# A fused attention and feed-forward kernel: a load, a set of copies and two value products change places

## The chip, the cores and the metric

The kernel runs on one core of a Trainium2 chip. The metric is device time in microseconds (us) of one execution; lower is better. Names of engines in the profile: PE is TensorE (matmuls; PEld its weight loads), DVE is VectorE, ACT is ScalarE, POOL is GpSimd, SP is SyncE. ACT, SP and Pool also issue transfers.

## The reference

Block-sorted attention over 4 batches, 8 heads, 768 positions and 64 features, and then a gated feed-forward layer on its output. Cut to what matters:

```python
P = sort_net                                   # (4, 8, 8, 8)
for _ in range(5):
    P = exp(P - max(P, -1)); P = P / (sum(P, -1) + 1e-9); P = P / (sum(P, -2) + 1e-9)
k_sorted = einsum('bhij,bhjcd->bhicd', P, k_blocks)      # 8 blocks of 96 positions
v_sorted = einsum('bhij,bhjcd->bhicd', P, v_blocks)
attn = softmax(q_blocks @ k_sorted.T / 8)                # inside each block
x = (attn @ v_sorted) as (3072, 512)
h = x @ w_in                                             # 512 -> 2048
out = (h * cos(h)) @ w_out                               # 2048 -> 512
```

## The kernel before

The work is cut into eight chunks of 384 tokens: chunk n is batch n // 2 and one half of its eight blocks. In a chunk the four blocks are `u` = 0 to 3. For each (n, u) the kernel calls `qk` (scores into PSUM; DVE takes the row maximum at L483 and subtracts it at L489), `expo` (ACT's exponential into one of three buffers `p_buf`, L507, then the transpose of the result: on PE for early chunks, otherwise by a transfer on SP's queue, L520), `av` (the value product on PE, L546; DVE divides by the sum, L553 and L555; the result is transposed by SP, L561, or on PE by `x_transpose`, L573). Then come `moe_up` (L597, with ACT's sine at L604 and DVE's product at L612) and `moe_down` (L629). The order of all instructions is written out by hand: each engine executes its own in that order, and the up and down products of one chunk carry, in slots between their matmuls, the attention calls of later chunks. `moe_down(n, slots, mid=...)` makes six halves of eight matmuls, e = 0 to 5; the calls in slot e follow half e, those in `mid[e]` stand behind its first four matmuls.

The head has an order of its own. Three loads bring the sort matrix into the tile `P_a` (L83 twice, L85 once); groups g = 0 and 1 are batches 0, 1 and 2, 3. DVE takes the maximum (L239), ACT the exponential (L240), and four rounds follow (`it` = 0 to 3): exponential on ACT (L330), a product with a mask on PE (`product`, L261), reciprocal and scaling on DVE (L350, L321, L324). Between the products of the rounds PE also transposes q of chunk 0 (`q_products`, `q_turn`, L299; 32 transposes, 16 in each of two PSUM tiles), which ACT copies out. At the end of the rounds `spread(0)` writes the sorting matrix `bds[0]` (L280). From it `k_sort_0` makes the sorted keys of chunk 0: per call some products on PE (L361) and four copies into `kT[0]`, of 8 or 16 columns per head, on DVE (V, L288) or ACT (A, L286). `v_turn` turns the matrix for the values (tile `bdv`), and `v_sort_b` sorts the values (L451).

Pool issues the loads of q, k, v and the weights (`load_q`, `load`, `load_w_in`, `load_w_out`), clears buffers and makes the identity (`make_identity`); it also permutes v (L176). PSUM tiles come from two pools: `big` with three buffers (B in the calls) and `acc` with two (C).

Of the kernel before, what the change touches and what calls it, by code (L numbers as in the profile page):

```python
# [18 lines left out]
def kernel(  # L19
# [15 lines left out]
    nc = tc.nc  # L35
    B, H, S, D = q.shape
# [26 lines left out]
    big = ctx.enter_context(tc.tile_pool(name="big", bufs=3, space=bass.MemoryType.PSUM))  # L63
# [7 lines left out]
    vbuf, kbuf = kv[:, :CD], kv[:, CD:]  # L71
# [10 lines left out]
    for r, b in ((64, 0), (0, 1)):  # L82
        (nc.scalar, nc.sync)[b].dma_start(  # L83
            out=P_a[r:r + 64, 0], in_=sort_net[b].rearrange("h i j -> (h i) j"))
    nc.scalar.dma_start(  # L85
        out=P_a[:, 1], in_=sort_net[2:].rearrange("b h i j -> (b h i) j"))

    kin_d = k.rearrange("b h (j c) d -> b (h j) (c d)", j=nb)
    vin_d = v.rearrange("b h (j c) d -> b (h j) (c d)", j=nb)

    def load(buf, r, src):
        nc.gpsimd.dma_start(out=buf[r:r + 64], in_=src)
# [16 lines left out]
    def q_zeroed(n):  # L109

        return kbuf[:blk, :2 * (QZ + D)] if n % 2 else q_mem[:]
# [7 lines left out]
    def load_q(n):  # L119
        b, ih = n // 2, n % 2  # L120
        if n < NQ:

            nc.gpsimd.dma_start(
                out=q_rows, in_=q[b][:, ih * IC * blk:(ih + 1) * IC * blk].rearrange(
                    "h (p r) d -> p h (r d)", r=QR))
        else:
            src = q[b].rearrange("h (i c) d -> c i h d", c=blk).rearrange(
                "c i (h e) d -> c i h e d", e=2)
            q_heads = q_zeroed(n).rearrange("p (e x) -> p e x", e=2)[:, :, :QZ].rearrange(
                "p e (i h w) -> p i h e w", i=IC, h=H2)[:, :, :, :, :D]  # L130
            for i in range(IC):
                for e in range(2):
                    nc.gpsimd.dma_start(  # L133
                        out=q_heads[:, i, :, e], in_=src[:, ih * IC + i, :, e])

    def q_of(n, e):
        return q_turned[n % 2][:, e]
# [17 lines left out]
    def load_w_in(z):  # L155
        c = slice(z * Dff // 4, (z + 1) * Dff // 4)
        nc.gpsimd.dma_start(out=w_in_t[:, :, c], in_=w_in_d[:, :, c])

    def load_w_out(z):
        c = slice(z * FC // 4, (z + 1) * FC // 4)  # L160
        nc.gpsimd.dma_start(out=w_out_t[:, c], in_=w_out_d[:, c])
# [22 lines left out]
    kTs = const.tile([128, 3, 3, NB, HT], BF16, name="kTs")  # L184
    kT, kT2 = [kTs[:, :, 0], kTs[:, :, 2]], kTs[:, :, :2]

    load_q(0)
    make_identity(nc, ident[:])
    load(kbuf, 64, kin_d[0])
    load(vbuf, 0, vin_d[0])  # L190
    NP = 3
    p_bufs = []
    for i in range(NP):
        t = const.tile([blk, 2 * H2, 128], BF16, name=f"p_buf{i}")
        nc.gpsimd.memset(t[:, :, blk:], 0.0)
        p_bufs.append(t)
    vS[0] = const.tile([blk, 4 * NB, VW], BF16, name="vS")
    vS[1] = pair[:blk].rearrange("p (x w) -> p x w", w=VW)

# [59 lines left out]
    def product(lhs, rhs):  # L259
        ps = acc.tile([128, nb], FP32, name="sk", tag="acc")  # L260
        nc.tensor.matmul(  # L261
            ps[:], lhs.rearrange("p x j -> p (x j)"), rhs, start=True, stop=True)
        return ps
# [15 lines left out]
    def spread(g):  # L279
        nc.vector.scalar_tensor_tensor(  # L280
            bds[g][:], maskp.to_broadcast([128, 2 * H, nb]), ci[g][:], along(T[g]),
            op0=ALU.mult, op1=ALU.mult)

    def copy_on(eng, dst, src):
        if eng is nc.scalar:
            eng.copy(dst, src)  # L286
        else:
            eng.tensor_copy(dst, src)  # L288

    V, A = nc.vector, nc.scalar  # L290
# [3 lines left out]
    def q_products(n, z, lo, hi, pool, tag):  # L294
        if lo == 0:
            q_ps[n, z] = pool.tile([128, 2, IC, QR, blk // QR], BF16, name="qps", tag=tag)
        for i in range(lo, hi):
            e, hp, r = i // (2 * QR), i // QR % 2, i % QR
            nc.tensor.transpose(  # L299
                q_ps[n, z][hp * D:(hp + 1) * D, e, :, r],  # L300
                q_rows[:, (z * 2 + e) * 2 + hp, r * D:(r + 1) * D], ident[:blk, :blk])

    def q_turn(n, z, pool, tag, lo=0):
        q_products(n, z, lo, 4 * QR, pool, tag)
        ps = q_ps.pop((n, z))

        def place(hp, rows):
            dst = q_of(n, hp)[rows, :QW].rearrange("d (i h c) -> d h i c", h=H2, c=blk)
            return dst[:, z * 2:z * 2 + 2], ps[rows].rearrange("d e i r p -> d e i (r p)")

        if n == 0:
            return [place(0, slice(0, 128))]
        return [place(hp, slice(hp * D, (hp + 1) * D)) for hp in range(2)]
# [5 lines left out]
    def balance(g):  # L319

        nc.vector.scalar_tensor_tensor(  # L321
            T_eps[g][:], E_eps[g][:], 1.0, rr_one[g][:], op0=ALU.mult, op1=ALU.mult,
            accum_out=cs[g][:])
        nc.vector.reciprocal(ci[g][:], cs[g][:])  # L324
# [3 lines left out]
    for it in range(4):  # L328
        for g in range(NG):
            nc.scalar.activation(E[g], T[g], AF.Exp, scale=ci[g][:])  # L330
        nc.vector.tensor_copy(seen[:], E[0][:, :1])
        if it == 3:
            copy_on(A, *turned[0])
        sk = [product(same, E[g]) for g in range(NG)]
        if it == 1:
            q_products(0, 0, 0, 10, big, "big")
        elif it == 2:
            turned = q_turn(0, 0, big, "big", 10)
            q_products(0, 1, 0, 4, big, "big")
        elif it == 3:  # L340
            turned = q_turn(0, 1, big, "big", 4)
            copy_on(A, *turned[0])
        if it == 1:

            nc.gpsimd.tensor_copy(held[:], cs[1][:])
            for z in range(3):
                load_w_in(z)
            load_w_out(0)
        for g in range(NG):
            nc.vector.reciprocal(rr[g], sk[g][:])  # L350
            if it < 3 or g == 0:
                balance(g)
                if it == 3:
                    spread(0)
# [5 lines left out]
    def k_products(ps, t, c, rows, rhs, keys=kbuf):  # L360
        nc.tensor.matmul(  # L361
            ps[:, t], keys[rows, c * 2 * D:(c + 1) * 2 * D], rhs, start=True, stop=True)

    def k_sort_0(t0, nt, eng, pool, tag):

        ps = pool.tile([128, nt, 2 * MH], FP32, name="ks", tag=tag)
        for t in range(nt):
            k_products(ps, t, t0 + t, slice(64, 128),
                       bds[0][64:, H:, :IC])
        ms, ts = slice(0, MH), slice(t0, t0 + nt)  # L370
        psv = ps.rearrange("p t (e m) -> p e m t", e=2)
        for hp in range(2):
            for x in range(2):
                copy_on(eng, kT[0][hp * D:(hp + 1) * D, hp + x, ms, ts],
                        psv[x * D:(x + 1) * D, hp])
# [58 lines left out]
    def v_turn(eng=A):  # L434
        ps = big.tile([128, 128], FP32, name="bdp", tag="big")
        for r in (0, 64):
            nc.tensor.matmul(
                ps[r:r + 64], ident[:, 64 - r:128 - r], bds[0].rearrange("p x i -> p (x i)"),
                start=True, stop=True)
        copy_on(eng, bdv.rearrange("p x i -> p (x i)"), ps[:])  # L440
# [217 lines left out]
    def moe_down(n, slots=(), stores=nc.sync, mid={}):  # L658

        for e in range(2 * TC // 128):  # L660
            down(n, e // 2, e % 2, stores, mid.get(e, ()))
            step(slots[e] if e < len(slots) else ())

    B, C = (big, "big"), (acc, "acc")
# [27 lines left out]
        next(wz)  # L692

    k_sort_0(40, 8, V, *B)
    k_sort_0(0, 16, V, *C)
    v_turn()
    load_q(1)
    k_sort_0(32, 8, V, *B)
    load_w_in(3)
    k_sort_0(16, 16, A, *B)  # L700
    v_sort_b(0, 0, 8, A, *B)
    load_w_out(1)
    qk(0, 0)
# [140 lines left out]
    def ahead(n, *more):  # L844
# [5 lines left out]
        for e, calls in more:  # L850
# [8 lines left out]
             mid={5: [(x_transpose, 3, 1, V, *B), (x_transpose, 3, 2, V, *B),  # L859
                  (x_transpose, 3, 3, V, *B)]})  # L860
# [13 lines left out]
             None, mid={5: [(x_transpose, 4, 3, A, *B)]})  # L874
# [5 lines left out]
               [(qk_half, 5, 2, 1)], [], [(qk, 5, 3)]])  # L880
    expo(5, 1)
    expo(5, 2)
    moe_down(4, [[(qk, 6, 0)], [(av, 5, 0), (expo, 5, 3)], [(qk, 6, 1)],
                 [(av, 5, 2), (expo, 6, 0)], [(av, 5, 3, True), (expo, 6, 1), (qk, 6, 2)]],
             None, mid={3: [(av, 5, 1)], 5: [(x_transpose, 5, 3, A, *B)]})
    q_transpose_dma(7)
# [6 lines left out]
             mid={5: [(x_transpose, 6, 3, A, *B)]})  # L893
# [1 line left out]
               [(qk_half, 7, 3, 1)]])  # L895
    expo(7, 2)
    expo(7, 3)
    moe_down(6, [[(av, 7, 0)], [(av, 7, 1)], [(av, 7, 2, True)], [(av, 7, 3, True)],
                 [(x_transpose, 7, 2, A, *B)]], None,
             mid={5: [(x_transpose, 7, 3, A, *B)]})  # L900
    moe_up(7, [[(let_go, 6, 0)], [(let_go, 6, 1)], [(let_go, 6, 2)]])
    for e in range(2 * TC // 128 - 2):
        down(7, e // 2, e % 2, nc.sync)
# [41 lines left out]
```

## Time and profile before

| | |
|---|---|
| median of 3 runs | 239.96 us (239.51 to 241.65) |
| profiled execution | 241.18 us, of which the span of the profile is 239.4 us |
| busy, share of the span | PE 226.0 us (94%), DVE 175.8 (73%), ACT 155.3 (65%), POOL 87.7 (37%) |
| transfers | 30.90 MB, mean 129 GB/s |
| granted clock of TensorE | 0.998 of full speed |

The profile is that of one execution. Times in its rows count from the start of the span. A row of the order in time gives start, length, engine, line, operation, tiles and count; in brackets stands the idle time of the engine before it, and what ended that. The chain of waits is followed back from the last instruction: at each step to what released it.

### The profile page before, as it was taken

Reading aid. Unit: us, or ns where it says so; the run is one execution under the profiler, and the core shown is the slowest. Engines: PE = TensorE matmul, PEld = TensorE weight load, DVE = VectorE, ACT = ScalarE, POOL = GpSimd, SP = SyncE. Lnnn points to the kernel's source line nnn. Section 1 sums busy time; section 2 is a strip of 40 time slices with the busy share of each in tenths; the row PEclk is TensorE's granted clock in tenths of the full one; section 3 lists DMA queues with packets and bytes.
Section 4 is the critical chain, followed back from the end, with each engine's and each line's share of the span. In section 5 each row is a group of like instructions: output and inputs, shape, how many; then the busy total and the mean of one; then the engine's idle time right before and its main releaser. Section 6 shows DMA issues by size and latency. Waiting matters only on the chain.

```text
span 239.4 us, 5344 instructions
## 1 busy us (share of the span) xinstructions
PE 226.0 (94%) x2148; PEld 148.1 (62%) x2169; DVE 175.8 (73%) x325; ACT 155.3 (65%) x217; POOL 87.7 (37%) x110
## 2 busy tenths in 40 slices
PE   2797999999999999999999999999999999999994
PEld 0777788956766566656566565655565566456554
DVE  3678977698879976895768986897789769635700
ACT  4355967785688946888578947683667376737611
POOL 6469953896960056990726200800000000000000
PEclk9999999999999999999999999999999999999999
DMA  6999999992999259786889769926671450251012
GB/s 82 213 198 205 207 210 219 212 158 89 132 152 162 66 138 191 122 179 154 117 115 126 79 136 140 189 43 99 136 212 33 102 181 0 49 140 44 0 47 89
DMA packets 66681, 30.90 MB, mean 129 GB/s; under 512 B 55392, under 2 KB 62176, under 8 KB 66400
## 3 DMA queue, kind: packets, MB, share of 16 engines
q0 software_dynamic: 24048, 13.64, 41.1%
q1 hardware_dynamic: 42096, 16.72, 29.8%
q8 instruction: 17, 0.28, 0.5%
q10 hardware_dynamic: 512, 0.20, 0.3%
q14 instruction: 8, 0.07, 0.1%
HBM read 27.27 MB, written 6.29 MB: 140 GB/s over the span
## 4 chain that ended last, share of the span: by engine, by line
PE 85%; DVE 7%; DMA 3%; ACT 2%; issue 1%; ACTq 0%; DVEq 0%
PE h L597 34%; PE o L629 31%; PE sc L428 4%; PE av L546 4%; PE ks L361 2%; DVE kTs L288 2%; PE xps L573 2%; PE pps L533 2%; PE vs L461 2%; DMA P_a<-in_sort_net_dram 2%; PE o L909 1%; PE sk L261 1%; PE qps L299 1%; DMA vperm<-p_buf 1%; PE vs L451 1%
## 5 line engine op out<-in xcount | busy, mean ns | idle before, releaser
L597 PE MATMUL h<-xT,w_in_t 128*128 128x384 bf16 (+1 forms) x576 | 91.2, 310 | 0.4 <-DVE xn L555 0.3
L629 PE MATMUL o<-w_out_t,gg 128*128 128x512 bf16 x347 | 85.1, 379 | 1.1
L604 ACT ACTIVATE c<-h,half_pi 128x768 f32<-128x768 f32 (+1 forms) x68 | 58.6, 864 | 26.8 <-PE h L597 25.6
L612 DVE TENSOR_TENSOR gg<-c,h 128x768 bf16<-128x768 f32 (+1 forms) x64 | 57.1, 899 | 22.2 <-ACT c L604 22.2
L597 PEld LDWEIGHTS <-w_in_t 128*128 128x128 bf16 x576 | 53.1, 98 | 27.1 <-issue 1.0
L629 PEld LDWEIGHTS <-gg 128*128 128x128 bf16 x368 | 33.1, 98 | 30.9
L489 DVE TENSOR_TENSOR s<-sc,mx 96x384 f32<-96x384 f32 (+1 forms) x43 | 32.2, 749 | 2.3
L483 DVE TENSOR_REDUCE mx<-sc 96x4 f32<-96x384 f32 (+1 forms) x43 | 31.9, 741 | 1.4 <-PE sc L428 0.7
L176 POOL COPY vperm<-kv 64x1536 bf16<-64x1536 bf16 (+1 forms) x10 | 28.0, 2843 | 1.1 <-DMA kv<-in_v_dram 1.1
L507 ACT ACTIVATE p_buf<-s 96x768 bf16<-96x768 f32 x32 | 26.0, 840 | 3.2 <-DVE s L489 2.9
L555 DVE TENSOR_TENSOR xn<-av,r 96x512 bf16<-96x512 f32 x32 | 22.0, 686 | 1.1
L133 POOL DMA_DIRECT2D kv<-in_q_dram x24 | 15.9, 671 | 0.8 <-issue 0.8
L428 PE MATMUL sc<-kTs,q_turned 128*128 128x96 bf16 x224 | 15.6, 206 | 0.0
L428 PEld LDWEIGHTS <-q_turned 128*128 128x128 bf16 x224 | 12.8, 98 | 4.0 <-DVE s L489 0.4
L553 DVE RECIPROCAL r<-av 96x8 f32<-96x8 f32 x32 | 6.4, 199 | 11.6 <-PE av L546 11.5
L286 ACT COPY kv<-o 128x512 f32<-128x512 f32 (+2 forms) x10 | 5.3, 531 | 14.3 <-PE o L629 12.7
L286 ACT CAST kTs<-ks 128x512 bf16<-128x512 f32 (+1 forms) x21 | 11.2, 539 | 3.7 <-PE ks L361 3.7
L133 POOL DMA_DIRECT2D q_mem<-in_q_dram x16 | 10.7, 684 | 2.6 <-DMA kv<-in_v_dram 2.3
L288 DVE COPY kv<-o 128x512 f32<-128x512 f32 (+1 forms) x5 | 3.0, 602 | 11.4 <-PE o L909 8.6
L286 ACT COPY xT<-xps 128x384 bf16<-128x384 bf16 (+1 forms) x10 | 5.1, 511 | 9.1 <-PE xps L573 9.1
L604 ACT ACT_TABLE_LOAD x8 | 10.3, 1283 | 0.1
L286 ACT COPY o_s<-o 128x512 f32<-128x512 f32 x9 | 5.3, 586 | 7.4 <-PE o L629 7.2
(105 smaller groups left out, 230.6 us busy)
## 6 DMA issues: line engine op xcount, KB each, us to landing
out_dram<-kv SPq DMA_DIRECT2D x12, 256.0 KB, 2.7
out_dram<-o_s SPq DMA_DIRECT2D x11, 256.0 KB, 2.4
w_in_t<-in_moe_w_in_dram POOLq DMA_DIRECT2D x4, 512.0 KB, 8.7
w_out_t<-in_moe_w_out_dram POOLq DMA_DIRECT2D x4, 512.0 KB, 12.6
kv<-in_k_dram POOLq DMA_DIRECT2D x2, 768.0 KB, 9.0
kv<-in_v_dram POOLq DMA_DIRECT2D x2, 768.0 KB, 12.5
pair<-in_k_dram POOLq DMA_DIRECT2D x2, 768.0 KB, 12.3
kv<-in_v_dram POOLq DMA_DIRECT2D x6, 256.0 KB, 6.3
```

The source lines that it names most:

```text
L133: nc.gpsimd.dma_start(out=q_heads[:, i, :, e], in_=src[:, ih * IC + i, :, e])
L176: nc.gpsimd.tensor_copy(dst, src)
L286: eng.copy(dst, src)
L428: nc.tensor.matmul(out, q_of(n, hp)[:, x:x + 128], keys_of(n, u, h2, hp), start=True, stop=True)
L483: nc.vector.reduce_max(mx[:], scv, axis=AX.X)
L489: nc.vector.tensor_tensor(s, scv, mx.to_broadcast(list(s.shape)), op=ALU.subtract)
L507: nc.scalar.activation(p[:, :, :blk], s_t.pop((n, u)).rearrange("p e h c -> p (e h) c"), AF.Exp, scale=scale)
L555: nc.vector.tensor_tensor(xn.rearrange("p h e d -> p e h d"), avv[:, :, :, :D], r.to_broadcast([blk, 2, H2, D]), op=ALU.mult)
L597: nc.tensor.matmul(to, w_in_t[:, kk, f * 128:(f + 1) * 128], xT[n][:, kk, lo:hi], start=(kk == 0), stop=(kk == KC - 1))
L604: nc.scalar.activation(c[:, :, :x], h[:, :, :x], AF.Sin, bias=half_pi[:, 0:1])
L612: nc.vector.tensor_tensor(gate(n, fp)[:, :, lo:hi], c[:, :, :x], h[:, :, :x], op=ALU.mult)
L629: nc.tensor.matmul(o[:], gate(n, f // 2)[:, f % 2, ts * 128:(ts + 1) * 128], w_out_t[:, f, :], start=(f == 0), stop=(f == FC - 1))
```

## The change

Five edits, none of which adds or removes arithmetic:

1. The third load of `P_a` is issued by SP, behind SP's first one, instead of ACT.
2. On Pool the identity and the clearing of the first `p_buf` come ahead of the loads of q, k and v; before, the q load came first.
3. The transposes of q for chunk 0 are spread over the rounds as 4, 12, 10, 6 instead of 0, 10, 10, 12.
4. The first keys: the order of the calls, and the engine and pool of some. `k_sort_0(32, 8)` copies on ACT and uses `acc`; the copy of `v_turn` moves from ACT to DVE, ahead of DVE's long key copies; Pool's order there stays as it was.
5. In the down product of chunk 4, `expo(5, 3)` comes ahead of `av(5, 0)`: on ACT, PE and DVE the order stays, on SP the transpose of the softmax now stands ahead of that of the value product. In the down product of chunk 6, `av(7, 2)` moves from behind half 2 into the middle of half 3.

```diff
-    nc.scalar.dma_start(
+    nc.sync.dma_start(
         out=P_a[:, 1], in_=sort_net[2:].rearrange("b h i j -> (b h i) j"))
...
-    load_q(0)
     make_identity(nc, ident[:])
-    load(kbuf, 64, kin_d[0])
-    load(vbuf, 0, vin_d[0])
     NP = 3
     p_bufs = []
     for i in range(NP):
         t = const.tile([blk, 2 * H2, 128], BF16, name=f"p_buf{i}")
         nc.gpsimd.memset(t[:, :, blk:], 0.0)
         p_bufs.append(t)
+        if i == 0:
+            load_q(0)
+            load(kbuf, 64, kin_d[0])
+            load(vbuf, 0, vin_d[0])
...
-        if it == 1:
-            q_products(0, 0, 0, 10, big, "big")
+        if it == 0:
+            q_products(0, 0, 0, 4, big, "big")
+        elif it == 1:
+            turned = q_turn(0, 0, big, "big", 4)
         elif it == 2:
-            turned = q_turn(0, 0, big, "big", 10)
-            q_products(0, 1, 0, 4, big, "big")
+            q_products(0, 1, 0, 10, big, "big")
         elif it == 3:
-            turned = q_turn(0, 1, big, "big", 4)
+            turned = q_turn(0, 1, big, "big", 10)
             copy_on(A, *turned[0])
...
     k_sort_0(40, 8, V, *B)
+    k_sort_0(16, 16, A, *B)
+    load_q(1)
+    v_turn(V)
+    load_w_in(3)
     k_sort_0(0, 16, V, *C)
-    v_turn()
-    load_q(1)
-    k_sort_0(32, 8, V, *B)
-    load_w_in(3)
-    k_sort_0(16, 16, A, *B)
+    k_sort_0(32, 8, A, *C)
     v_sort_b(0, 0, 8, A, *B)
...
-    moe_down(4, [[(qk, 6, 0)], [(av, 5, 0), (expo, 5, 3)], [(qk, 6, 1)],
+    moe_down(4, [[(qk, 6, 0)], [(expo, 5, 3), (av, 5, 0)], [(qk, 6, 1)],
                  [(av, 5, 2), (expo, 6, 0)], [(av, 5, 3, True), (expo, 6, 1), (qk, 6, 2)]],
              None, mid={3: [(av, 5, 1)], 5: [(x_transpose, 5, 3, A, *B)]})
...
-    moe_down(6, [[(av, 7, 0)], [(av, 7, 1)], [(av, 7, 2, True)], [(av, 7, 3, True)],
+    moe_down(6, [[(av, 7, 0)], [(av, 7, 1)], [], [(av, 7, 3, True)],
                  [(x_transpose, 7, 2, A, *B)]], None,
-             mid={5: [(x_transpose, 7, 3, A, *B)]})
+             mid={3: [(av, 7, 2, True)], 5: [(x_transpose, 7, 3, A, *B)]})
```

## The prediction

> **What bounds the kernel now.** I read the first and fourth part of the page, then the busy time by stage, then the chain of waits and the order in time of the stages that the change touches.
>
> ```profile
> span 239.4 us, 5344 instructions
> PE 85%; DVE 7%; DMA 3%; ACT 2%; issue 1%; ACTq 0%; DVEq 0%
> 0.00:5.00 5.00, 1.46 (x3) 0.28 (x3) 1.29 (x9) 1.77 (x4) 3.83 (x13) 1.00 0.40 44
> 156.00:169.00 13.00, 12.69 (x113) 6.74 (x113) 11.57 (x18) 7.62 (x11) 0.00 (x0) 1.00 0.40 70
> ```
>
> TensorE holds 85% of the chain that ended last. In a late stage, 156 to 169, it is busy for 12.69 us of 13 (first figure behind the length), so a wait removed there is worth tenths of a microsecond. The head is different: in 0 to 5 us TensorE has 1.46 us, of mere warming up. There a serial chain sets the end: a load of the sort matrix, four rounds of normalising on DVE, ACT and PE, then the copies of the first sorted keys. Whatever shortens it moves all that follows, unless a load is late there.
>
> ```profile
> 1.36 3.64 DMA P_a<-in_sort_net_dram
> 1.36 0.86 ACTq L85 DMA_DIRECT2D P_a<-in_sort_net_dram  x1
> 1.30 0.90 POOL L123 DMA_DIRECT2D q_mem<-in_q_dram  x1 [0.85 <-POOLq L929]
> 2.50 0.29 POOL masks.py:199 TENSOR_SCALAR_AFFINE_SELECT ident<-ident 128x128 bf16<-128x128 bf16 x1
> 3.79 0.34 POOL L195 MEMSET p_buf<- 96x256 bf16 x1
> P_a<-in_sort_net_dram SPq DMA_DIRECT2D x1, 2.0 KB, 2.1
> ```
>
> The head waits for the third load of the sort matrix: issued at 1.36, it lands 3.64 later, at 5.00. The load of half as many rows on SP's queue lands 2.1 after its issue.
>
> **The change part by part.**
>
> *Third sort load, later q load.* Packets by queue in two short stretches, 3.4 to 3.7 and 4.0 to 4.3 us, show why the third load is slow. It has 144 packets on ACT's queue (q10); q0 is Pool's, with the q load.
>
> ```profile
> q0 software_dynamic: 44, 0.02, 72.9%
> q10 hardware_dynamic: 15, 0.00, 6.9%
> q0 software_dynamic: 59, 0.03, 74.6%
> q10 hardware_dynamic: 57, 0.00, 22.9%
> ```
>
> Its packets pass between those of the q load, and few pass before 4 us. In the change Pool first makes the identity and clears one buffer, then issues the q load. Pool's first row after the start stands at 1.30; the identity fills the time from the end of the q issue, 2.20, to 2.79, the buffer takes 0.34: so the q issue moves to about 2.2, by 0.9. If Pool is free before 1.30 it moves by less, down to about 0.4. SP can issue the third load behind its own first one, for the same 0.86, so no sooner than ACT did. On SP the first load was issued at 0.74 for 0.58 and landed at 2.84, 1.5 after the issue ended. With the same 1.5 and, as an estimate, 0.35 for 64 more rows the third lands at 2.2+1.5+0.35 = 4.05, 0.95 before. I take 0.9. Lower bound: 0, if it stays as slow; a loss is left out, since it starts no later and what competes with it starts later. Upper bound: 1.3, set by q, below. I stay near the estimate because the q load's packets would then start when most of the 144 are through.
>
> By the Trainium skill (DMA: Bandwidth & Descriptors, "Issuing engines are not separate DMA queues") transfers from SP, ACT and Pool run on the same 16 engines and interleave, so another issuing engine saves issue time only. The packet rows agree that they interleave. By that rule the move to SP brings nothing by itself, and all of the 0.9 hangs on the later q load; the sum without it is that of rival 1.
>
> *Transposes of q.* The 32 transposes go 4, 12, 10 and 6 into the four rounds, where they went 0, 10, 10 and 12.
>
> ```profile
> 7.63 1.06 PE L261 MATMUL sk<-E,same 128*128 128x8 f32 x4 [0.40 <-ACT E L330]
> 9.33 1.18 PE L261 MATMUL sk<-E,same 128*128 128x8 f32 x4 [0.64 <-ACT E L330]
> 14.08 0.78 PE qps L299 x12
> 14.15 0.35 DVE L280 SCALAR_TENSOR_TENSOR bd<-maskp,ci,T 128x128 bf16<-128x128 f32 x1
> 14.79 0.82 PE L361 MATMUL ks<-bd,kv 64*128 64x32 bf16 x24
> DMA to landing us min/median/max: 5.6/5.6/5.6
> DMA to landing us min/median/max: 2.4/4.2/10.5
> ```
>
> One costs 0.065 us. Round 1 gets two more, and the product behind them comes 0.13 later. The last round gets six fewer, 0.39: they end at 14.08+0.13+0.39 = 14.60, the spread matrix is there at 14.50+0.13 = 14.63, so the key products start at about 14.70 in place of 14.79. Net 0.1 (between -0.2 and 0.3). The four in round 0 lie in PE's slack of 0.64 before 9.33, if q has landed. Its load (the first of the two landing rows) takes 5.6: 2.2+5.6 = 7.8, while with 0.9 won the products of round 0 end at 8.69-0.9 = 7.8 too. The products of round 1, then due at 8.4, follow the four at 0.26 behind q; so q is just in time, each 0.1 beyond 8.15 costs 0.1, and with q at 7.8 they can't start before 8.05: that caps the first term at 1.3.
>
> *First keys.* The scores wait for every copy into the key tile.
>
> ```profile
> 15.22 4.18 DVE L288 CAST kTs<-ks 64x128 bf16<-64x128 f32 x12 [0.60 <-PE ks L361]
> L288 DVE CAST kTs<-ks 64x128 bf16<-64x128 f32 x8 | 2.3, 289 | 0.7 <-PE ks L361 0.6
> L288 DVE CAST kTs<-ks 64x256 bf16<-64x256 f32 x4 | 1.7, 422 | 0.1
> 14.89 0.80 ACT L286 COPY q_turned<-qps 128x768 bf16<-128x768 bf16 x1 [0.78 <-PE qps L299]
> 15.90 0.27 ACT L286 CAST bdv<-bdp 128x128 bf16<-128x128 f32 x1 [0.20 <-PE bdp L437]
> 16.84 1.50 ACT L286 CAST kTs<-ks 64x256 bf16<-64x256 f32 x4 [0.68 <-PE ks L361]
> 20.94 0.59 ACT L286 CAST vS<-vs 96x512 bf16<-96x512 f32 x1 [1.99 <-PE vs L451]
> ```
>
> DVE has twelve copies in a row, 15.22 to 19.40, while ACT has gaps. The change gives four short ones to ACT and takes the copy of bdv from it. DVE then: start 15.12, four short 1.20, bdv 0.29 (DVE's row for 128 columns), four long 1.72, end 18.33. ACT: the q copy starts when the transposes end and is over at about 15.42, four long 1.50, four short at between 0.27 (its bdv) and 0.37 (its long ones), end 18.1 to 18.4. So the scores start at about 18.35 instead of 19.40: 1.05 with the 0.1 above. Bounds: 0.7, if the four short ones on ACT need half as much again as its long ones, and 1.2. What ACT has behind them, the copies of v, is covered by its wait of 1.99 before 20.94; without that cover the 1.1 to 1.5 of the four would lie on its way to the first softmax.
>
> *Chunk 5.* Only SP's order changes: the transpose of the last softmax stands ahead of that of a value product.
>
> ```profile
> 162.69 1.21 SPq L561 DMA_TRANSPOSE xT<-xn  x1
> 164.00 2.62 DMA vperm<-p_buf
> 164.62 1.89 PE L629 MATMUL o<-w_out_t,gg 128*128 128x512 bf16 x8
> 166.66 0.32 PEld L546 LDWEIGHTS <-vperm 96*128 96x128 bf16 x8 [0.64 <-DMA vperm<-p_buf]
> 167.27 1.03 PE L629 MATMUL o<-w_out_t,gg 128*128 128x512 bf16 x4
> ```
>
> It is issued at 164.00 and lands 2.62 later, with PE waiting. Issued at 162.69 it lands at 165.3. What PE loses: from one group at L629 to the next are 2.65 us, where eight matmuls and a value product take 1.98 (205.23 to 207.21 in the next fence) and the scores between, eight matmuls, some 0.34: 0.33. I take 0.3; bounds 0, if it lands as late behind the two ahead of it, and 0.64. The value product's transpose comes 1.3 later, at 164.0; its reader is the next up-projection, behind 169, which covers it.
>
> *Chunk 7.* The third value product moves behind four matmuls.
>
> ```profile
> 205.23 1.89 PE L629 MATMUL o<-w_out_t,gg 128*128 128x512 bf16 x8
> 207.21 1.89 PE L629 MATMUL o<-w_out_t,gg 128*128 128x512 bf16 x8
> 209.14 0.32 PEld L546 LDWEIGHTS <-vperm 96*128 96x128 bf16 x8 [0.53 <-DMA vperm<-p_buf]
> 209.41 1.89 PE L629 MATMUL o<-w_out_t,gg 128*128 128x512 bf16 x7
> ```
>
> From 207.21 to 209.41 are 2.20 instead of 1.98: 0.2 is lost to the late transpose, and four matmuls, half of 1.7, will cover it. Its own reader follows more than eight matmuls later. I take 0.2; bounds 0 and 0.53.
>
> *Sum.* 0.9+1.05+0.3+0.2 = 2.45. The profiled execution took 241.18 (span 239.4 and 1.78 around it) and would take 238.7. The median of the runs, 239.96, is 1.22 below it; the same 2.45 from it gives 237.5.
>
> **The rivals.**
>
> 1. *The third load stays as slow.* For it: the q load's packets were slow before 4 us as well, so the start itself may be slow, and SP issues no sooner. Against it: half the rows landed in 2.1. Time: 237.5+0.9 = 238.4.
>
> 2. *A load takes the head's gain back.* The compute comes 1.95 sooner, the loads don't.
>
> ```profile
> 17.48 2.74 POOL L176 COPY vperm<-kv 64x1536 bf16<-64x1536 bf16 x1
> 23.80 1.19 PE L451 MATMUL vs<-bdv,vperm 64*128 64x64 bf16 x16
> 45.52 5.65 POOL L176 COPY vperm<-kv 64x1536 bf16<-64x1536 bf16 x2 [1.13 <-DMA kv<-in_v_dram]
> ```
>
> For it: the second v already comes late to Pool, at 45.52. Against it: four such copies end near 57 and the first product that reads them comes after 60. The first v, permuted by 20.22, is read at 23.80: 1.6 of slack remain, or 0.7 if v lands 0.9 later with q. If it fails all the same, the whole 1.95 is lost: 239.4.
>
> 3. *Slower: PE's queue stands behind the four transposes of round 0.* PE takes its work in order; if q is late, the products of round 1 wait, and with them DVE and ACT. They stood at 9.33, so the whole change loses once they start after 9.33+1.55 = 10.9, that is when q lands after 10.6, 8.4 after its issue. The longest landing on the same tile is 10.5 (the second landing row, of all its loads), but 5.6 was this load's. At 10.5 the products start at 12.95: 3.6-1.55 = 2.05 slower, 242.0.
>
> 4. *All terms at their upper ends*: 1.3+1.2+0.64+0.53 = 3.65, 236.3. For it: 0.64 and 0.53 are what the weight loads stood idle. Against it: PE's own rows show half of that.
>
> **How the numbers follow.** Forecast 237.5, chance 0.55, its own range 236.7 to 238.2. Rival 1: 0.15. Rival 2: 0.08. Rival 3: 0.05. Rival 4: 0.17. The runs shown spread from 239.51 to 241.65, so 1%, 2.4 us, is about what a measurement tells from no change; that border, 237.56, goes through the middle of the forecast. Faster by over 1%: rival 4 and 0.33 of the forecast, 0.50. Slower by over 1%: rival 3 and a little for bounds that fail, 0.06. The rest, 0.44, is within 1%. The range from 236.0 to 239.6 takes in rivals 1, 2 and 4 and leaves out rival 3 and the far ends.
>
> **What would show it.** Right: the second maximum of the sort matrix (DVE) at about 4.1; the products of round 1 at about 8.4; key copies that end together on ACT and DVE, and the scores in full near 17.5; no idle time of the weight loads ahead of the value products that waited at 166.66 and 209.14. Wrong: the third load still landing near 5; transposes of round 0 that start after 8.2; scores that wait for ACT's copies; or a gain of 2 us at 20 us that is gone at 60.

## The result and the profile after

| | before | after |
|---|---|---|
| median of the runs beside each other | 239.96 us (239.51 to 241.65, 13 runs) | 238.54 us (238.03 to 239.04, 13 runs) |
| ratio after / before | | 0.9923 [0.9902, 0.9945] |
| profiled execution | 241.18 us, span 239.4 | 238.29 us, span 236.5 |

The kernel is faster, by 0.8%: less than the 1% that the prediction took for its border, and 1.0 us less of a gain than the 237.5 it gave. The two profiled executions lie further apart, 2.89 us, than the two medians, 1.42. Most of what follows is about that difference.

Lines of the changed kernel count one or two higher than those of before (L546 is now L548). First the head, from the timeline of after (start, length, engine, line, operation, tiles, count, and in brackets the idle time before it and what ended that):

```profile
0.75 0.20 POOL masks.py:197 MEMSET ident<- 128x128 bf16 x1 [0.29 <-POOLq L931]
1.40 0.82 SPq L85 DMA_DIRECT2D P_a<-in_sort_net_dram  x1
1.51 0.91 POOL L123 DMA_DIRECT2D q_mem<-in_q_dram  x1
3.23 0.36 DVE L240 TENSOR_REDUCE nmx<-P_a 128x1 f32<-128x8 f32 x2 [1.13 <-DMA P_a<-in_sort_net_dram]
7.21 0.34 PEld L300 LDWEIGHTS <-q_mem 96*64 96x64 bf16 x4 [0.22 <-DMA q_mem<-in_q_dram]
7.73 1.18 PE L262 MATMUL sk<-E,same 128*128 128x8 f32 x4
13.10 0.80 PE L363 MATMUL ks<-bd,kv 64*128 64x32 bf16 x24
13.93 2.60 ACT L287 CAST kTs<-ks 64x256 bf16<-64x256 f32 x8
14.94 1.74 DVE L289 CAST kTs<-ks 64x256 bf16<-64x256 f32 x4
16.73 0.87 PE L425 MATMUL sc<-kTs,q_turned 64*96 64x96 bf16 x15 [0.47 <-DVE kTs L289]
```

The issues of the loads, with the microseconds to their landing in the last column:

```profile
q_mem<-in_q_dram POOLq DMA_DIRECT2D x1, 384.0 KB, 5.7
P_a<-in_sort_net_dram SPq DMA_DIRECT2D x1, 4.0 KB, 2.0
```

The third load lands at 1.40+2.0 = 3.4, where the prediction's row had 5.00, and the two maxima now run as one group that is over at 3.59. The products of round 1 start at 7.73 (9.33 before), the key products at 13.10 (14.79), the copies end together on DVE (16.68) and ACT (16.53), and the scores start in full at 16.73. In the profile of before the second maximum, that row of the scores, the starts of the up products of chunks 1, 3, 5 and 7, and that of the down product of chunk 6 (L629) are these (two rows of the timeline, then rows of the chain of waits, which give start, length, engine, tile, line and count):

```profile
5.03 0.16 DVE L239 TENSOR_REDUCE nmx<-P_a 128x1 f32<-128x8 f32 x1 [1.87 <-DMA P_a<-in_sort_net_dram]
19.45 0.80 PE L423 MATMUL sc<-kTs,q_turned 64*96 64x96 bf16 x15 [0.25 <-DVE kTs L288]
...
64.59 1.41 PE h L597 x8
145.25 3.90 PE h L597 x24
169.33 3.90 PE h L597 x24
203.46 1.67 PE o L629 x7
215.36 10.40 PE h L597 x64
```

and in the chain of after:

```profile
61.94 1.41 PE h L599 x8
142.59 3.90 PE h L599 x24
156.45 4.32 DMA vperm<-p_buf
166.59 3.97 PE h L599 x24
200.79 1.67 PE o L631 x7
212.48 10.40 PE h L599 x64
```

The scores come 2.72 us sooner, in three parts. The second maximum starts 1.60 sooner (5.03 before; 3.23+0.36-0.16 = 3.43 after). From it to the key products are 9.67 instead of 9.76, so 0.09 comes from the transposes of q. From there to the scores are 3.63 instead of 4.66, so 1.03 comes from the copies of the first keys.

Of the 2.72, 2.65 are left at chunk 1, 2.66 at chunk 3, 2.74 at chunk 5, 2.67 at the down product of chunk 6 and 2.88 at chunk 7. So the head's gain goes through to the end, chunk 7 adds 0.2, and chunk 5 nothing that lasts. A wait for a transposed softmax, 4.32 us from issue to landing, stands in the chain of after there.

**Two groups of runs before.** In all, 74 runs of the kernel before stood beside those of after and of the experiments: 48 lie between 239.43 and 240.40 (median 239.82), 26 between 241.01 and 242.31 (median 241.47), none between 240.40 and 241.01. The profiled execution of before, 241.18, belongs to the smaller group. After has one group. A profile shows one group only, so that of before couldn't tell what sets them 1.65 us apart. The granted clock of TensorE was 0.997 to 1.000 in every run, so it is not the clock.

### The profile page after: what moved, and what is told of

Read it like the earlier page. It is cut to its first block, busy times and chain, and to the rows that moved or that the text cites. A ratio compares the mean times of both kernels' runs of the same rounds, so it can differ in the third digit from the quotient of the medians.

```text
span 236.5 us, 5344 instructions
## 1 busy us (share of the span) xinstructions
PE 226.3 (96%) x2148; PEld 148.3 (63%) x2169; DVE 174.8 (74%) x322; ACT 155.9 (66%) x220; POOL 87.9 (37%) x110
## 3 DMA queue, kind: packets, MB, share of 16 engines
q1 hardware_dynamic: 42240, 16.73, 29.6%
## 4 chain that ended last, share of the span: by engine, by line
PE 85%; DVE 5%; DMA 4%; ACT 3%; issue 1%; POOL 0%; POOLq 0%; ACTq 0%
PE h L599 35%; PE o L631 30%; PE av L548 4%; PE sc L430 3%; PE ks L363 3%; DMA q_mem<-in_q_dram 2%; DMA vperm<-p_buf 2%; PE xps L575 2%; PE pps L535 2%; PE vs L463 2%; PE o L911 1%; PE qps L300 1%; PE sk L262 1%; PE vs L453 1%; DVE s L491 1%
## 5 line engine op out<-in xcount | busy, mean ns | idle before, releaser
L287 ACT CAST kTs<-ks 128x512 bf16<-128x512 f32 (+2 forms) x25 | 12.2, 494 | 3.2 <-PE ks L363 3.0
L606 ACT ACT_TABLE_LOAD x8 | 10.3, 1283 | 0.1
```

What stands on the lines that cost most here:

```text
L606: nc.scalar.activation(c[:, :, :x], h[:, :, :x], AF.Sin, bias=half_pi[:, 0:1])
```

## The experiments

**What decides the landing of the third load?** Theory T: the packets of the load that Pool issued, if they come ahead of the third load's, hold it up; the later q issue prevents that, and the two groups of before are executions in which the one or the other came first. Its rival: the queue decides, that is, SP's queue is quicker than ACT's second load. Four kernels on one chip; 27 runs of the kernel before beside them had a median of 240.16.

*b_again*: the kernel before, unchanged.

> The kernel before, unchanged, for a second profile. Its thirteen times lie in two groups, nine from 239.5 to 240.2 and four from 241.2 to 241.7, and the execution profiled first took 241.18. Theory T (a race at the start: the third sort load is slow only when the q load's packets reach the transfer engines ahead of it): both groups show again, and a profile of the lower group has the third load landing 1 to 1.6 us sooner than 5.00, its scores starting at about 18. Rival S (the queue: ACT's second load is always slow): the third load lands near 5.0 in either group, and the groups differ elsewhere.

Measured: 240.14 us, 0.9986 [0.9955, 1.0018]; seven runs from 239.55 to 240.16 and three from 241.14 to 241.55. Its profiled execution took 241.26 and shows the landing of 3.6 again, the second maximum at 5.02. Two profiles of the upper group agree; the lower group had no profile yet.

*a_act*: the changed kernel with the third load back on ACT.

```diff
-    nc.sync.dma_start(
+    nc.scalar.dma_start(
         out=P_a[:, 1], in_=sort_net[2:].rearrange("b h i j -> (b h i) j"))
```

> The changed kernel with the third sort load back on ACT's queue; Pool's order as changed. Theory T: the q load is still issued after it (1.5 against 1.36), so the load lands before 4.0 in most executions and the time is 238.5 to 238.9. Rival S: it lands near 5.0 as it did on ACT's queue, the normalising starts 1.6 later, and the time is 239.8 to 240.2.

Measured: 238.42 us (238.06 to 238.78), 0.9911 [0.9875, 0.9947]; from the group of its tile:

```profile
L85 ACTq DMA_DIRECT2D P_a<-in_sort_net_dram x1: 597/597/597, 1.3 to 1.3; - x1
DMA to landing us min/median/max: 1.8/2.0/2.2
```

On ACT's queue the load lands 1.8 after its issue, at least as quick as on SP. The move to SP earns nothing. By the Trainium skill's rule (DMA: Bandwidth & Descriptors, "Issuing engines are not separate DMA queues") it shouldn't, and this run agrees.

*a_qfirst*: the changed kernel with Pool's old order, the third load left on SP.

```diff
+    load_q(0)
     make_identity(nc, ident[:])
+    load(kbuf, 64, kin_d[0])
+    load(vbuf, 0, vin_d[0])
...
-        if i == 0:
-            load_q(0)
-            load(kbuf, 64, kin_d[0])
-            load(vbuf, 0, vin_d[0])
```

> The changed kernel with Pool's old order (q load first, at about 1.30); the third sort load stays on SP. Theory T: the q load's packets start with or ahead of those of the third load, which lands between 4 and 5; the time is 239.2 to 240, perhaps in two groups. Rival S: on SP it lands at 3.4 whatever Pool does, q lands 0.2 sooner, and the time is 238.3 to 238.6.

Measured: 239.85 us, 0.9958 [0.9926, 0.9991]; three runs from 238.24 to 238.59, seven from 239.66 to 240.24. The timeline of its profiled execution, 240.07:

```profile
1.30 0.90 POOL L123 DMA_DIRECT2D q_mem<-in_q_dram  x1 [0.85 <-POOLq L930]
1.39 0.83 SPq L85 DMA_DIRECT2D P_a<-in_sort_net_dram  x1
5.29 0.16 DVE L239 TENSOR_REDUCE nmx<-P_a 128x1 f32<-128x8 f32 x1 [1.88 <-DMA P_a<-in_sort_net_dram]
```

The load is slow on SP too, and the two groups are back, about 1.5 us apart. Pool's order decides whether there is an upper group, not the queue. Whether the queue shifts its share (seven of ten here, 26 of 74 before) is open with so few runs. The q issue stands only 0.21 us earlier than in after.

*b_loads*: the kernel before with edits 1 and 2 alone.

```diff
-    nc.scalar.dma_start(
+    nc.sync.dma_start(
         out=P_a[:, 1], in_=sort_net[2:].rearrange("b h i j -> (b h i) j"))
...
-    load_q(0)
     make_identity(nc, ident[:])
...
+        if i == 0:
+            load_q(0)
+            load(kbuf, 64, kin_d[0])
+            load(vbuf, 0, vin_d[0])
```

> The kernel before with the two edits of the loads alone (third sort load on SP, q load behind the identity and one cleared buffer). The prediction gave these two 0.9 us; the two profiles gave 1.6. Theory T: 0.2 to 0.5 off the lower group and 1.6 off the upper, so one group at 239.3 and a median 0.6 lower than before. Rival S: 1.6 off every execution: 238.3.

Measured: 239.80 us (239.54 to 240.42, ten runs in one group), 0.9983 [0.9959, 1.0008]; the load lands in 2.1, the scores stand at 17.98. The loads' edits remove the upper group and leave the lower one where it was: 239.80 against 239.82. The 0.2 to 0.5 that the expectation also took off the lower group did not come. The edits are worth about 1.6 us in one execution of three, and nothing in the others.

**Is the lower group of before the one with a quick load?** *b_again2*, the kernel before once more, for a profile of that group, and *a_kfirst*, the test from the other side: the changed kernel in which Pool issues the k load first of all. Rows of k are longer than those of q (12 KB against 0.5 KB), and the load is twice as large (768 KB against 384). 15 runs of the kernel before beside these two and n_sp had a median of 240.29.

> The kernel before once more, for a profile of its lower group of times (two of three executions). Theory T: an execution of 239.4 to 240.4 has its third sort load landing at 3.3 to 4.0 instead of 5.00 and its scores starting near 17.9; from there to the end the same 219.9 to 220.1 as before. If the execution is again of the upper group, it shows 5.0 and tells nothing new.

Measured: 239.85 us in the one run, in the lower group. Its timeline:

```profile
1.29 0.90 POOL L123 DMA_DIRECT2D q_mem<-in_q_dram  x1 [0.83 <-POOLq L929]
1.35 0.60 ACTq L85 DMA_DIRECT2D P_a<-in_sort_net_dram  x1
...
3.35 0.16 DVE L239 TENSOR_REDUCE nmx<-P_a 128x1 f32<-128x8 f32 x1 [0.16 <-DMA P_a<-in_sort_net_dram]
```

and the packets by queue in two short stretches, 2.5 to 2.8 and 2.8 to 3.1 us (q10 is ACT's queue, with the third load; q0 is Pool's; columns: packets, MB, share of 16 engines):

```profile
q10 hardware_dynamic: 123, 0.00, 20.5%
q0 software_dynamic: 11, 0.01, 24.5%
q10 hardware_dynamic: 21, 0.00, 3.5%
```

Here the same program has the third load at 3.35. ACT's issue took 0.60 instead of the 0.86 in the prediction's row, and 123 of the 144 packets went before the first of q0. This is theory T inside the kernel before: two profiles of the upper group have the load late, the one of the lower group has it early. In after the issue on SP takes 0.82 and the 144 packets go from 2.8 to 3.1, but q0 comes later still, from 3.1 to 3.4:

```profile
q1 hardware_dynamic: 144, 0.00, 24.0%
q0 software_dynamic: 21, 0.01, 41.0%
```

So there are two ways to be first: a shorter issue, seen in the one profile of the lower group of before, or a q load 0.2 us later, which after has always. That all executions of the lower group had the shorter issue is likely, but not shown; why it takes 0.60 one time and 0.86 another stays open.

*a_kfirst* differs from after in this:

```diff
+    load(kbuf, 64, kin_d[0])
     make_identity(nc, ident[:])
...
             load_q(0)
-            load(kbuf, 64, kin_d[0])
             load(vbuf, 0, vin_d[0])
```

> The changed kernel with Pool's k load issued first, at about 1.3, where the old order had q; identity, one cleared buffer, q and v follow. Theory T in its wide form (any transfer of Pool whose packets come first holds the third sort load): it lands at 4 to 5 in most executions. In its narrow form (the 768 short rows of q hold it, the 64 long rows of k hardly do): it lands below 4. In both, q queues behind k and lands later than 7.8, so that PE's four transposes of round 0 make the head wait: this prices the prediction's rival 3, 1 us for each us of q beyond about 7.3. Time 239 to 242.

Measured: 243.68 us (243.45 to 244.04), 1.0111 [1.0054, 1.0169], slower. Timeline, and the packets from 2.5 to 2.8 (a share over 100% means that packets which last longer than the stretch are counted whole):

```profile
1.26 0.66 POOL L92 DMA_DIRECT2D kv<-in_k_dram  x1 [0.81 <-POOLq L931]
1.39 0.57 SPq L85 DMA_DIRECT2D P_a<-in_sort_net_dram  x1
8.49 0.16 DVE L240 TENSOR_REDUCE nmx<-P_a 128x1 f32<-128x8 f32 x1 [5.41 <-DMA P_a<-in_sort_net_dram]
...
q0 software_dynamic: 9, 0.11, 295.6%
```

Nine packets of k, 0.11 MB, are ahead, and a load of 4 KB lands 7.1 us after its issue although that took only 0.57. The second maximum comes 5.1 us after that of the changed kernel (8.49 against 3.43), and the median is 5.1 longer, against after as against n_sp on this chip: the head passes on what it loses one to one. So a short issue alone is no protection: what counts is whose packets come first. Whether the longer rows of k or its larger size make the difference to q was not taken apart. The q load lands at 10.3 in this kernel and binds nothing there, so rival 3 of the prediction was not priced by it.

**What are the other edits worth?** Three kernels, each the changed one with one edit undone, and one tried as an improvement, on a chip where 19 runs of the kernel before had a median of 239.86.

*a_keys_old*: edit 4 undone.

```diff
     k_sort_0(40, 8, V, *B)
-    k_sort_0(16, 16, A, *B)
-    load_q(1)
-    v_turn(V)
-    load_w_in(3)
     k_sort_0(0, 16, V, *C)
-    k_sort_0(32, 8, A, *C)
+    v_turn()
+    load_q(1)
+    k_sort_0(32, 8, V, *B)
+    load_w_in(3)
+    k_sort_0(16, 16, A, *B)
```

> The changed kernel with the first keys in their old order (edit 4 undone: eight short and four long copies in a row on DVE, the copy of bdv on ACT). Theory K (the keys carry nearly all that is left when the third load is fast): the scores start about 1.0 later than in the changed kernel, at 17.7, and the time is 239.4 to 239.6. Rival U (the transposes of q carry it, since PE then finishes them sooner): the scores start 0.4 later at most, and the time is 238.7 to 238.9.

Measured: 239.37 us (239.15 to 239.86), 0.9966 [0.9943, 0.9989]. Timeline:

```profile
13.53 4.18 DVE L289 CAST kTs<-ks 64x128 bf16<-64x128 f32 x12 [0.44 <-PE ks L363]
17.77 0.80 PE L425 MATMUL sc<-kTs,q_turned 64*96 64x96 bf16 x15 [0.25 <-DVE kTs L289]
```

DVE has its twelve copies in a row again, and the scores come at 17.77 instead of 16.73: 1.04 later. By the medians it is 0.83 over after, which had no runs on this chip, and 0.98 over a_tp_old, which had.

*a_tp_old*: edit 3 undone.

```diff
-        if it == 0:
-            q_products(0, 0, 0, 4, big, "big")
-        elif it == 1:
-            turned = q_turn(0, 0, big, "big", 4)
+        if it == 1:
+            q_products(0, 0, 0, 10, big, "big")
         elif it == 2:
-            q_products(0, 1, 0, 10, big, "big")
+            turned = q_turn(0, 0, big, "big", 10)
+            q_products(0, 1, 0, 4, big, "big")
         elif it == 3:
-            turned = q_turn(0, 1, big, "big", 10)
+            turned = q_turn(0, 1, big, "big", 4)
```

> The changed kernel with the old spread of the q transposes (0, 10, 10, 12). Theory K, by the prediction's 0.1: first key products 0.1 later, 238.6. The trace of the changed kernel also shows a q load that lands at 7.17 just ahead of the four transposes of round 0; without them this wait goes, so that the net may be nothing: 238.5. Rival U: the six extra transposes of the last round hold the keys for their full 0.4: 238.9.

Measured: 238.39 us (238.29 to 238.86), 0.9910 [0.9876, 0.9944]; key products at 12.92 and scores at 16.58, no later than in after. But in this execution the issue of the third load took 0.57 us, 0.82 in after, and the head started sooner:

```profile
3.16 0.16 DVE L240 TENSOR_REDUCE nmx<-P_a 128x1 f32<-128x8 f32 x1 [0.17 <-DMA P_a<-in_sort_net_dram]
12.92 0.82 PE L362 MATMUL ks<-bd,kv 64*128 64x32 bf16 x24
```

From the second maximum to the key products are 9.76 here, as in the profile of before (and in b_loads), and 9.67 in after, a_keys_old, a_tail_old and n_best. So the edit is worth 0.09 us, the prediction's 0.1; the medians can't show so little. In a_act the second maximum comes at 3.17 and this stretch is 9.74: there the transposes of round 0 wait 0.28 for q and start at 7.09.

*a_tail_old*: edit 5 undone, both parts.

```diff
-    moe_down(4, [[(qk, 6, 0)], [(expo, 5, 3), (av, 5, 0)], [(qk, 6, 1)],
+    moe_down(4, [[(qk, 6, 0)], [(av, 5, 0), (expo, 5, 3)], [(qk, 6, 1)],
...
-    moe_down(6, [[(av, 7, 0)], [(av, 7, 1)], [], [(av, 7, 3, True)],
+    moe_down(6, [[(av, 7, 0)], [(av, 7, 1)], [(av, 7, 2, True)], [(av, 7, 3, True)],
                  [(x_transpose, 7, 2, A, *B)]], None,
-             mid={3: [(av, 7, 2, True)], 5: [(x_transpose, 7, 3, A, *B)]})
+             mid={5: [(x_transpose, 7, 3, A, *B)]})
```

> The changed kernel with both edits of the down products undone. By the prediction's terms (0.3 and 0.2): 0.5 slower, 239.0, with weight loads idle for 0.6 ahead of av(5, 3) and 0.5 ahead of av(7, 2). By the two profiles already seen, where the shift between them grows by 0.1 over chunk 5's stage and by 0.2 over chunk 7's: 0.2 to 0.3 slower, 238.8.

Measured: 238.64 us (238.59 to 239.10), 0.9925 [0.9897, 0.9954]: 0.1 over after, inside the spread of either, and 0.25 over a_tp_old on the same chip. The trace tells the parts from each other. From the first down product of chunk 6 to the up product of chunk 7 are 215.36-203.46 = 11.90 us before, 11.90 here, and 212.48-200.79 = 11.69 in after: 0.21 for chunk 7. From the first down product of chunk 4 to that of the next chunk are 24.08 before, 24.10 here, 24.08 in after and 24.00 in a_act: at most 0.1 for chunk 5.

*n_best*: a_act, with the value product (5, 1) moved back behind half 3, so that its late transpose is covered.

```diff
-                 [(av, 5, 2), (expo, 6, 0)], [(av, 5, 3, True), (expo, 6, 1), (qk, 6, 2)]],
-             None, mid={3: [(av, 5, 1)], 5: [(x_transpose, 5, 3, A, *B)]})
+                 [(av, 5, 1), (av, 5, 2), (expo, 6, 0)], [(av, 5, 3, True), (expo, 6, 1), (qk, 6, 2)]],
+             None, mid={5: [(x_transpose, 5, 3, A, *B)]})
```

> The changed kernel with the third sort load on ACT's queue and av(5, 1) moved behind half 3 of the down product of chunk 4, next to av(5, 2), so that four more matmuls cover the transpose that lands 4.3 us after its issue. If the wait that remains at 160.8 (0.65 idle on the weight loads) is a real loss of about 0.3: 238.1 to 238.2. If a later wait takes its place (the transposes of the value products are issued 0.8 later and the next up product reads them): 238.4 to 238.8.

Measured: 238.29 us (238.09 to 238.62), 0.9910 [0.9875, 0.9944]. The idle time of weight loads that wait for a transposed softmax falls from 0.9 in after to 0.2, and the next up product starts no sooner: the chain of waits names SP's last transpose, issued at 164.05 and landing 2.31 later, and the product follows at 166.49. Its interval overlaps those of a_act and after: no version here is shown to beat the changed kernel.

**Why was chunk 5 worth nothing?** Theory Q: SP's queue of six transposes decides when the next up product starts, in whatever order they stand. The rival: something else ends at nearly the same time. SP's queue in the stage, before:

```profile
159.10 3.49 SPq L520 DMA_TRANSPOSE vperm<-p_buf  x2
162.69 1.21 SPq L561 DMA_TRANSPOSE xT<-xn  x1
164.00 1.23 SPq L520 DMA_TRANSPOSE vperm<-p_buf  x1
165.36 2.48 SPq L561 DMA_TRANSPOSE xT<-xn  x2
```

and after:

```profile
156.45 4.91 SPq L522 DMA_TRANSPOSE vperm<-p_buf  x3
161.45 3.81 SPq L563 DMA_TRANSPOSE xT<-xn  x3
```

From the first issue to the end of the last are 8.74 and 8.81 us, 8.76 in a_tail_old, 8.73 in a_act and 8.80 in n_best; the weight loads of the up product follow 1.2 us later in each (at 169.04 before, 166.48 after). The other way to the up product, over PE's transposes and ACT's copy of them, ends 0.06 ahead of these loads before, 0.23 in after and 0.54 in n_best: it moves, and the start doesn't. The first of the six lands late in both kernels, 4.1 to 4.3 us after its issue, and in before too a weight load, that of av(5, 1), waited for it:

```profile
163.23 0.32 PEld L546 LDWEIGHTS <-vperm 96*128 96x128 bf16 x8 [0.41 <-DMA vperm<-p_buf]
```

*n_sp* takes one transpose away from SP: a_act with the transposed value product (5, 2) made on PE, together with (5, 3).

```diff
-                 [(av, 5, 2), (expo, 6, 0)], [(av, 5, 3, True), (expo, 6, 1), (qk, 6, 2)]],
-             None, mid={3: [(av, 5, 1)], 5: [(x_transpose, 5, 3, A, *B)]})
+                 [(av, 5, 2, True), (expo, 6, 0)], [(av, 5, 3, True), (expo, 6, 1), (qk, 6, 2)]],
+             None, mid={3: [(av, 5, 1)], 5: [(x_transpose, 5, 2, A, *B, 3)]})
```

> The changed kernel with the third sort load on ACT's queue and the value product av(5, 2) transposed on PE, together with that of av(5, 3), instead of by SP. In all kernels so far the six transposes that SP issues in chunk 5's stage take 8.7 to 8.8 us from first issue to the end of the last, and the weight loads of the next up product start 1.2 us after that end, whichever of the six comes first. Theory Q (SP's queue is the limit of that stage, so reordering it gains nothing): with five, the up product starts as soon as PE gets there, 0.2 to 0.4 sooner than in a_act counted from the start of the down product; time 238.1 to 238.3. Rival: the value products themselves are the limit (the loads' idle time ahead of them), the up product starts at the same distance, and PE's extra transposes add 0.2: 238.6.

Measured: 238.55 us (238.18 to 239.11), 0.9913 [0.9883, 0.9943]. Its timeline:

```profile
160.67 3.13 SPq L563 DMA_TRANSPOSE xT<-xn  x2
165.84 0.80 ACT L287 COPY xT<-xps 128x768 bf16<-128x768 bf16 x1 [1.73 <-PE xps L575]
166.69 3.35 PEld L599 LDWEIGHTS <-w_in_t 128*128 128x128 bf16 x21 [0.30 <-issue]
```

SP is through at 163.80 now, 1.46 sooner than in after, but the weight loads (all but one) start at 166.69, behind ACT's copy of the part that PE transposed, which ends at 166.64. In after that copy, shorter, ended at 166.25. From the first weight loads of this down product to those of the next are 24.34 us here, 24.07 in after and 24.00 in a_act. So the gain that theory Q gave for this kernel did not come, and the time is the rival's 238.6. SP's queue sets the end of the stage in after, by two tenths; behind it the way over PE and ACT is the next limit, and here the moved transpose made that way longer. Relieving SP without loading PE and ACT was not tried.

## Why the prediction was right and wrong

- **What bounds the kernel: right.** The head is a serial chain, and what shortens it moves the whole: 2.72 us at the scores, 2.65 at 62 us, 5.1 for 5.1 in a_kfirst. Every sign that the prediction named as right appears in the profile, those with a time 0.7 to 0.8 us sooner than stated (the second maximum at 3.43 for 4.1, round 1 at 7.73 for 8.4, the scores at 16.73 for 17.5). Rival 2, a load that takes it back, didn't occur, but the slack is gone: weight loads wait 0.2 for the permuted v in after, and 0.4 in a_act, whose head is 0.2 quicker still.
- **Third sort load, 0.9: the mechanism was right, its base was wrong.** It was taken from one execution and then subtracted from the median of the runs. In the execution that was profiled it brought 1.6 (5.00 to 3.4), more than the term; in two executions of three the load was quick already, and there it brings nothing (b_loads: 239.80 against 239.82). The step that failed is "the same 2.45 from it gives 237.5". Of the three times on hand, 239.51, 239.96 and 241.65, two lay over a microsecond below the profiled 241.18, which had warned of it. From the lower group's 239.82, 1.03 for the keys, 0.09 for the transposes and 0.21 for chunk 7 give 238.49; measured were 238.54, outside the forecast's own 236.7 to 238.2 and inside the whole range. The nearest of the five cases is rival 1 with 238.4, and that is luck: the third load did not stay slow, it had been quick already in most executions of before.
- **The shift of the q issue, 0.9 with 0.4 as the lower end: too large.** Pool was free well before 1.30: in after the identity starts at 0.75, and q went from 1.30 to 1.51. That 0.21 was enough, since what counts is which packets are first, and in after the packets of the third load are through by 3.1, just as those of q begin. The prediction had no row for how small a shift would do; that this one did was luck. The early q is also why the term could pass 1.3: that cap was worked out with q at 7.8, and q landed at 7.2.
- **SP in place of ACT, nothing: right** (a_act).
- **Transposes of q, 0.1: right**, 0.09 from the second maximum to the key products (a_tp_old). The q load landed at 1.51+5.7 = 7.2, just in time as said, with 0.22 of idle weight loads.
- **First keys, 1.05 with the 0.1 of the transposes: right.** 1.03 and 0.09 in the profiles. Four short copies on ACT took 2.60-1.50 = 1.10, the lower of the two prices, and DVE and ACT end 0.15 apart.
- **Chunk 5, 0.3: wrong, 0.1 at most.** The failed step is "its reader is the next up-projection, behind 169, which covers it". That reader was waiting for just this queue: the value products' transposes end 1.2 us ahead of it whatever stands in front. The wait at 166.66 did go. The other one, ahead of the value product (5, 1), which the prediction did not price, is 0.41 in the profile of before and 0.65 in after; a_act, with the same order, has 0.43, so it is not the edit's. What PE lost in the middle, it would have lost at the end.
- **Chunk 7, 0.2: right**, 0.21, and no weight load waits for the moved product.
- **Rivals 3 and 4** did not come: q was not late, and no term but the first one, in an execution of the upper group, reached its upper end.

## What to carry to other kernels

Look at the single times before a wait is priced from one profile: a gap among them says that the profile shows one of two executions, and a gain that removes the slower one moves the median less than it moves the profile. Where a serial head hangs on a small load, let its packets go ahead of large loads from other queues; here an issue two tenths of a microsecond too early cost 1.6 us in some executions, and a load twice as large with longer rows cost 5. And before a wait in the middle of a stage is priced, look for what the stage's last product waits for: if it is the same queue, the order inside the queue is worth nothing.

## What the runs showed of the hardware

A load of 4 KB landed 1.8 to 2.1 us after its issue when its packets went first, 3.6 to 3.9 behind the first packets of the q load, and 7.1 behind those of the k load. The issue of this load took 0.57 to 0.60 us in six of the thirteen profiled executions and 0.82 to 0.86 in seven, on ACT's queue as on SP's. In the three profiles of the kernel before it went with the time of the whole kernel: 0.60 in the execution of 239.85, 0.86 in those of 241.18 and 241.26. In chunk 5's stage the first of the transposes on SP's queue landed 4.1 to 4.3 us after its issue in both kernels, where the prediction's row had 2.62 for a later one; no run here says why.
